# Swapping the queues of the two last stores, and loading the second weights in three pieces: a gated mix of a state-space scan and an MLP on one core

## The chip, the core and the metric

The kernel runs on one core of one Trainium2 chip. The metric is device microseconds of one execution. Executions of the same kernel in one comparison lie up to about 1.4 us apart (0.7%), and 2.3 us in one kernel of the experiments, so each comparison was run in rounds, with the kernel before and the new one in turn on the same chip. Ratios are the mean time of one kernel's fast runs over the mean of the other's in the same rounds, so they are not quite the ratio of the medians quoted beside them.

## The reference

`x` has 2048 rows of 640. Cut to what matters, with two parts and a gate per row:

```python
g = sigmoid((x * gate_w).sum(-1, keepdims=True))
a = ssm(x, Lambda, B, C, dt, Dskip)          # complex diagonal scan over 2048 rows, 640 states
b = gelu(x @ w1 + b1) @ w2 + b2              # 640 -> 1728 -> 640
out = g * a + (1 - g) * b                    # bfloat16, 2048 x 640
```

## The kernel before

The rows are worked in four chunks of 512. In each chunk TensorE makes the scan's inputs (`ssm`), the first MLP layer (`ff1`), the second MLP layer (`fin_b`) and the scan's output projection (`fin_a`). Loads are issued up front on the SP queue, in one long line; the load of the second weights `w2_sb` (the profile drops digits and calls it `w_sb`) is one instruction in that line:

```python
    nc.sync.dma_start_transpose(out=BT_re[:], in_=A_B_re[:, :])
    nc.sync.dma_start_transpose(out=BT_im[:], in_=A_B_im[:, :])
    nc.sync.dma_start_transpose(out=xT[1][:], in_=x2d[CH:2 * CH, :])
    nc.sync.dma_start_transpose(out=CT_re[:], in_=A_C_re[:, :])
    nc.sync.dma_start_transpose(out=CT_im[:], in_=A_C_im[:, :])
    nc.sync.dma_start(out=w2_sb[:, 0:KF - 1, :], in_=B_w2[0:(KF - 1) * P, :].rearrange("(kf p) d -> p kf d", p=P))
    # ... rest of w2 and b2, Dbc ...
    nc.sync.dma_start_transpose(out=xT[2][:], in_=x2d[2 * CH:3 * CH, :])
    nc.sync.dma_start_transpose(out=xT[3][:], in_=x2d[3 * CH:4 * CH, :])
    load_xn(0, H, TPC)
    load_xn(1)
```

The second layer reads it in 14 slices `kf`, one after the other (`fin_b`):

```python
            for d0, d1 in HALVES:
                p = bank()
                for kf in range(KF):
                    m = P if kf < KF - 1 else F_LAST + 1
                    nc.tensor.matmul(p[:, 0:d1 - d0], lhsT=gel[c][:m, kf, lo:lo + P], rhs=w2_sb[:m, kf, d0:d1],
                                     start=(kf == 0), stop=(kf == KF - 1))
```

The last output tile is cut into columns 0 to 320, 320 to 512 and 512 to 640, so that its end can leave early (`fin_a`). The first two cuts go out as one store of 128 KB, the last as one of 32 KB:

```python
                dve_now(ck.pe + 0.2, 0.45, f)          # f: the eviction, ot = bank * gate + gb
                if ti == NT - 1 and i > 0:
                    s0 = 0 if i == 1 else d0
                    q = nc.sync if i == 1 else nc.scalar
                    q.dma_start(out=out2d[ti * P:(ti + 1) * P, s0:d1], in_=ot[:, s0:d1])
```

Some terms first. An eviction is the instruction, of VectorE or ScalarE, that takes a finished result out of TensorE's bank; the last one of the kernel is VectorE's. A landing is the moment when the last increment of a DMA's completion semaphore is recorded. A drain is an instruction that reads and writes no tile; the closing part has some on every engine, and in the experiments empty ones are added to SP.

DMAs take their completion semaphore in turn from a small set, whichever queue they are on. After the program's last line there is a closing part that the framework adds: SP waits in a fixed order for the last DMA on each semaphore, and then all engines meet in two barriers.

## Time and profile before

| | before |
|---|---|
| device time, median of 3 runs | 217.63 us (217.43 to 217.79) |
| span in the profile | 216.2 us |
| TensorE busy | 211.9 us, 98% of the span |
| end of the last eviction to the end of the span | 2.66 us |

The stretches first. The columns are the stretch and its length, then the busy time of each engine with its number of instructions, the granted TensorE clock, the DMA engines' mean share, and GB/s:

```profile
core 0: us, PE busy (x) PEld busy (x) DVE busy (x) ACT busy (x) POOL busy (x), PEclk, DMA share, GB/s
22.50:213.20 190.70, 190.66 (x1228) 115.45 (x1228) 172.41 (x341) 76.37 (x130) 0.00 (x0) 1.00 0.24 59
```

TensorE is busy for 190.66 of these 190.70 us at full granted clock. Nothing that any other engine or a DMA does in this stretch can cost time unless it makes TensorE wait. The chain of work that ended last (start, length, what), shortened:

```profile
9.85 5.63 SPq L139
15.48 0.04 issue
15.52 6.92 DMA BT_im<-in_A_B_im_dram
22.45 0.05 issue
22.49 9.89 PE bank L478 x45
...
202.27 10.91 PE bank L544 x90
213.17 0.03 issue
213.20 0.35 DVE ot L549
```

Up to 22.45 us the chain is the SP queue's issues and the landing of BT_im; then it is TensorE to 213.17 us, and one eviction. The chain's list stops there, at 213.55 us; the span goes on to 216.21. That rest is the last store and the closing part.

The SP queue around the load of the second weights (L144):

```profile
30.03 0.58 SPq L144 DMA_DIRECT2D w_sb<-in_B_w_dram  x1
...
32.60 8.86 SPq L148 DMA_TRANSPOSE xT<-in_A_x_dram  x1
41.50 3.12 SPq L149 DMA_TRANSPOSE xT<-in_A_x_dram  x1
44.66 1.09 SPq L117 DMA_DIRECT2D xn<-in_A_x_dram  x2
45.88 1.20 SPq L299 DMA_TRANSPOSE gel<-gelN  x1
```

The load's semaphore is full at 39.3 us by the trace's landing records; its first reader runs at 57.65 us. The two last stores:

```profile
212.64 0.91 DVE L549 SCALAR_TENSOR_TENSOR ot<-bank,gcol,gb 128x192 bf16<-128x192 f32 x2 [0.27 <-PE bank L544]
212.72 0.44 PE L544 MATMUL bank<-CT_im,hs 128*128 128x128 bf16 x5
213.09 0.33 SPq L556 DMA_DIRECT2D out_dram<-ot  x1
213.58 0.38 ACTq L556 DMA_DIRECT2D out_dram<-ot  x1
```

The last instructions of SP, grouped by line (engine, operation and number; shortest, median and longest duration in ns; first and last start), and from the page the packets by which instructions are fetched:

```profile
L612 SPq EVENT_SEMAPHORE  x7: 17/28/28, 213.5 to 216.1; - x7
L612 SPq DRAIN  x3: 7/12/13, 215.3 to 216.0; - x3
```

```profile
q14 instruction: 5, 0.04, 0.1%
```

### The profile page before, as it was taken

How to read it: one execution, taken by the hardware profiler on the slowest of the kernel's cores; microseconds unless marked ns; L12 is line 12 of the kernel's file. 1: busy time of each engine (PE TensorE's matmuls, PEld its weight loads, DVE VectorE, ACT ScalarE, POOL GpSimd, SP SyncE). 2: the span in 40 equal slices, each digit the busy share in tenths (PEclk: the TensorE clock that was granted, in tenths of full speed). 3: DMA queues.
4: the chain of work that ended last, by engine and by line, in shares of the span. 5: the costliest groups of instructions: out<-in, count | busy, mean ns of one | idle time of the engine just before them, and what ended most of it. 6: DMA issues, size and time to landing. Idle time of an engine off the chain costs nothing.

```text
span 216.2 us, 3470 instructions
## 1 busy us (share of the span) xinstructions
PE 211.9 (98%) x1368; PEld 128.2 (59%) x1368; DVE 189.8 (88%) x393; ACT 91.7 (42%) x156; POOL 1.6 (1%) x12
## 2 busy tenths in 40 slices
PE   7999999999999999999999999999999999999994
PEld 3855444454577775444477777444457777777773
DVE  3889999999999899999999999999999999961152
ACT  3689456675696101556642200456662210022100
POOL 2000000000000000000000000000000000000000
PEclk9999999999999999999999999999999999999999
DMA  5999999995000042000010006100001000100011
GB/s 174 255 224 199 226 214 369 175 246 103 3 0 0 0 141 106 0 0 3 0 24 3 0 0 200 45 2 0 0 3 24 0 3 30 61 30 3 2 61 61
DMA packets 32339, 16.16 MB, mean 75 GB/s; under 512 B 25091, under 2 KB 32324, under 8 KB 32324
## 3 DMA queue, kind: packets, MB, share of 16 engines
q1 hardware_dynamic: 32114, 15.91, 30.2%
q8 instruction: 10, 0.16, 0.3%
q10 hardware_dynamic: 210, 0.04, 0.1%
q14 instruction: 5, 0.04, 0.1%
HBM read 7.24 MB, written 2.62 MB: 46 GB/s over the span
## 4 chain that ended last, share of the span: by engine, by line
PE 88%; SPq 5%; DMA 5%; issue 0%; DVE 0%
PE bank L525 28%; PE bank L544 20%; PE bank L478 20%; PE bank L267 19%; DMA BT_im<-in_A_B_im_dram 3%; SPq L139 3%; DMA xn<-in_A_x_dram 1%; SPq L127 1%; SPq L125 1%; PE bank L292 1%; SPq L124 0%; SPq L138 0%; DVE ot L549 0%
## 5 line engine op out<-in xcount | busy, mean ns | idle before, releaser
L525 PE MATMUL bank<-w_sb,gel 128*128 128x320 bf16 x448 | 61.6, 299 | 0.0
L525 PEld LDWEIGHTS <-gel 128*128 128x128 bf16 x448 | 43.6, 98 | 17.2
L481 ACT ACTIVATE bu<-bank 128x512 bf16<-128x512 f32 x40 | 23.9, 597 | 41.7 <-PE bank L478 41.7
L271 ACT ACTIVATE gel<-bank,colB 128x512 bf16<-128x512 f32 x52 | 34.6, 693 | 15.1 <-PE bank L267 14.8
L544 PEld LDWEIGHTS <-hs 128*128 128x128 bf16 x330 | 31.8, 98 | 11.9
L434 DVE TENSOR_TENSOR_SCAN g<-r_c,carry,v 128x512 bf16<-128x512 f32 x30 | 37.2, 1270 | 0.0
L528 ACT ACTIVATE gb<-bank,gcol 128x320 f32<-128x320 f32 x32 | 16.5, 527 | 48.2 <-PE bank L525 46.6
L267 PE MATMUL bank<-xT,w1b 128*128 128x512 bf16 x140 | 31.0, 379 | 0.0
L267 PE MATMUL bank<-xT,w1a 128*128 128x512 bf16 (+1 forms) x150 | 27.6, 344 | 0.0
L544 PE MATMUL bank<-CT_im,hs 128*128 128x320 bf16 (+2 forms) x165 | 27.1, 295 | 0.0
L544 PE MATMUL bank<-CT_re,hs 128*128 128x320 bf16 (+2 forms) x165 | 27.1, 295 | 0.0
L549 DVE SCALAR_TENSOR_TENSOR ot<-bank,gcol,gb 128x320 bf16<-128x320 f32 (+2 forms) x33 | 17.3, 533 | 9.5 <-PE bank L544 9.3
L478 PE MATMUL bank<-xT,BT_im 128*128 128x512 bf16 x100 | 24.9, 379 | 0.1
L478 PE MATMUL bank<-xT,BT_re 128*128 128x512 bf16 x100 | 24.8, 379 | 0.0
L267 PEld LDWEIGHTS <-w1b 128*128 128x128 bf16 x140 | 13.6, 98 | 16.3 <-DMA w1b<-in_B_w_dram 0.3
L267 PEld LDWEIGHTS <-w1a 128*128 128x128 bf16 x150 | 14.9, 100 | 11.7
L511 DVE TENSOR_TENSOR bank<-xn,Dbc 128x320 f32<-128x320 bf16 (+2 forms) x33 | 14.3, 483 | 5.8 <-ACT gb L528 5.8
L478 PEld LDWEIGHTS <-BT_im 128*128 128x128 bf16 x100 | 9.7, 98 | 12.2 <-DMA BT_im<-in_A_B_im_dram 0.6
L478 PEld LDWEIGHTS <-BT_re 128*128 128x128 bf16 x100 | 9.7, 98 | 11.0
L415 DVE TENSOR_TENSOR v<-wa,wb 128x512 bf16<-128x512 bf16 x40 | 15.2, 421 | 0.7
L415 DVE TENSOR_TENSOR wa<-TCOS,g 128x1024 bf16<-128x1024 bf16 x20 | 13.7, 686 | 0.1
L415 DVE TENSOR_TENSOR wb<-TSIN,g 128x1024 bf16<-128x1024 bf16 x20 | 13.7, 684 | 0.0
(98 smaller groups left out, 130.7 us busy)
## 6 DMA issues: line engine op xcount, KB each, us to landing
out_dram<-ot SPq DMA_DIRECT2D x15, 160.0 KB, 1.8
w_sb<-in_B_w_dram SPq DMA_DIRECT2D x1, 2080.0 KB
xn<-in_A_x_dram SPq DMA_DIRECT2D x3, 640.0 KB, 4.9
w1b<-in_B_w_dram SPq DMA_DIRECT2D x5, 240.0 KB, 4.2
w1a<-in_B_w_dram SPq DMA_DIRECT2D x5, 192.0 KB, 3.5
xn<-in_A_x_dram SPq DMA_DIRECT2D x2, 320.0 KB
Dbc<-in_A_Dskip_dram SPq DMA_DIRECT2D x1, 160.0 KB
out_dram<-ot SPq DMA_DIRECT2D x1, 128.0 KB
```

The lines of the kernel that those rows point to most:

```text
L139: nc.sync.dma_start_transpose(out=BT_re[:], in_=A_B_re[:, :])
L267: nc.tensor.matmul(p[:, t0:t1], lhsT=w, rhs=xT[c][:, kd, t0:t1], start=(kd == 0), stop=(kd == KD - 1))
L271: nc.scalar.activation(out=gel[c][:, kf, :], in_=p[:, :], func=ACT.Gelu_apprx_tanh, bias=b1_c[:, kf:kf + 1])
L415: nc.vector.tensor_tensor(out=o, in0=a, in1=b, op=op)
L434: nc.vector.tensor_tensor_scan(s["g"][:, ri, :], r_c[:, ks:ks + 1].to_broadcast([P, CH]), s["v"][:, ri, :], init, ALU.mult, ALU.add)
L478: nc.tensor.matmul(p[:], lhsT=BT[:, kd, ks * P:(ks + 1) * P], rhs=xT[c][:, kd, :], start=(kd == 0), stop=(kd == KD - 1))
L481: nc.scalar.activation(out=bu[:, ri, :], in_=p[:], func=ACT.Identity)
L511: dve_now(ck.pe, 0.45, lambda: nc.vector.tensor_tensor(out=p[:, 0:d1 - d0], in0=xn[c][:, a, d0:d1], in1=Dbc[:, d0:d1], op=ALU.mult))
L525: nc.tensor.matmul(p[:, 0:d1 - d0], lhsT=gel[c][:m, kf, lo:lo + P], rhs=w2_sb[:m, kf, d0:d1], start=(kf == 0), stop=(kf == KF - 1))
L528: nc.scalar.activation(out=gb[:, d0:d1], in_=p[:, 0:d1 - d0], func=ACT.Identity, scale=gcol[:, 1, ti:ti + 1])
L544: nc.tensor.matmul(p[:, 0:d1 - d0], lhsT=hs[c][:, j, lo:lo + P], rhs=CT[:, j % KS, d0:d1], start=False, stop=(j == 2 * KS - 1), skip_group ...
L549: nc.vector.scalar_tensor_tensor(out=ot[:, d0:d1], in0=p[:, 0:d1 - d0], scalar=gcol[:, 0, ti:ti + 1], in1=gbs[ti][:, d0:d1], op0=ALU.mult, ...
```

## The change

The intent: the last store, which ends the kernel, should leave from the queue with the cheaper issue; and the second weights should arrive piece by piece, so that a reader of the first slices need not wait for the last.

```diff
-    nc.sync.dma_start(out=w2_sb[:, 0:KF - 1, :], in_=B_w2[0:(KF - 1) * P, :].rearrange("(kf p) d -> p kf d", p=P))
+    for k0, k1 in ((0, 4), (4, 8), (8, KF - 1)):
+        nc.sync.dma_start(out=w2_sb[:, k0:k1, :], in_=B_w2[k0 * P:k1 * P, :].rearrange("(kf p) d -> p kf d", p=P))
...
-                    q = nc.sync if i == 1 else nc.scalar
+                    q = nc.scalar if i == 1 else nc.sync
```

## The prediction

> What bounds the kernel now. TensorE. The table of stretches gives it 190.66 us busy of the 190.70 us from 22.5 to 213.2 us, at a granted clock of 1.00; the chain of waits is TensorE alone from 22.49 to 213.17 us. Before that the chain is the first load and the SP queue's issues (L124 to L139) up to the landing of the transposed BT_im at 22.45 us. After it come a 0.35 us VectorE eviction, the last store and the closing handshake, to 216.2 us.
>
> Second weights. The one load (2080 KB) is issued at 30.03 us and takes 0.58 us of the SP queue. In the packet records its packets run from about 32 to 39 us and its semaphore is full at 39.4 us. The first matmul that reads it starts at 57.65 us: 18 us of slack, and the list of waits has no wait of TensorE for it. Three pieces move the same bytes in the same packets and add two issues; a plain load of 240 to 640 KB takes 0.37 to 0.55 us of the queue here, so my estimate is +0.6 us of SP issue time (0.5 to 1.0). Behind it stand the third and fourth xT (needed at 84 and 135 us), xn tiles, and the last gel tile of chunk 0, issued at 45.88, landed at about 50.2 and read at about 59.5 us: nine us of slack against 0.6. The third xT transpose holds the queue for 8.86 us because the second weights drain in front of it (the fourth took 3.12), so part of the added issue time disappears there. The chain up to 22.45 us is issued before this load and can't move. New TensorE waits for pieces two and three are for semaphores long full. Worth: 0.0 us.
>
> Swap of queues. Now the 128 KB piece goes out on SP at 213.09 us (issue 0.33 us; first packet after 0.83 us, last at 214.45), and the 32 KB piece on ACT at 213.58 us (issue 0.38 us; first packet after 0.89 us, last at 214.75; semaphore full at 215.09). The end follows that landing by 1.1 us. The Trainium skill ("DMA: Bandwidth & Descriptors", section "Issuing engines are not separate DMA queues") says that DMAs of both issuers run on the same 16 engines and that several issuers save only issue time; the trace agrees as far as both queues' packets follow without a gap (SP's last at 214.45, ACT's first at 214.48). So the swap moves only issue costs: the piece that ends the kernel gets the issue that is 0.05 us shorter, and starts about 0.06 us earlier; the large piece ends about 214.51, so the two now overlap by about 0.1 us on shared engines, which eats part of it. Worth: -0.05 to 0.0 us.
>
> Sum: 217.63 - 0.03 + 0.0 = 217.6 us. The three runs of before spread over 0.36 us, more than the effect. Range 217.1 to 218.2. Chances: faster by over 2% 0.01, within 2% 0.98, slower 0.01.
>
> What would show it right: TensorE gapless from 22.5 to 213.2 us; no wait on the second weights; the third xT's issue 0.5 to 1 us later but its landing within 1 us of before; the last store's issue on SP 0.33 us, landing near 215.05 us; span 216.1 to 216.3 us. Wrong: a TensorE wait at 57.6 or 59.5 us, or the 32 KB piece landing after 215.2 us.
>
> What would make it wrong: the two added loads shift which earlier DMA a later one shares its semaphore with, or the scheduler's order of loads and stores on SP, so that an issue waits near the end; or a large store issued from ACT starts much later than from SP.

## The result, and the profile after

| | before | after |
|---|---|---|
| device time, median of 4 runs each | 217.71 us | 217.95 us (217.77 to 218.27) |
| ratio, 95% interval | | 1.0012 (0.9994 to 1.0031) |
| span in the profile | 216.2 us | 216.5 us |
| end of the last eviction | 213.55 us | 213.62 us |
| from there to the last landing | 1.54 us | 1.49 us |
| from there to the end of the span | 2.66 us | 2.87 us |

The last two rows disagree: counted from the end of the last eviction, the last store landed 0.05 us earlier, and the kernel ended 0.21 us later.

The stretches after:

```profile
22.50:213.20 190.70, 190.16 (x1219) 115.45 (x1228) 172.38 (x340) 76.38 (x130) 0.00 (x0) 1.00 0.24 59
```

The 0.50 us of busy time that seem lost are nearly all not waits: 9 of the 1228 matmul records are missing from this trace (the weight loads, x1228 in both, are complete). In the chain each missing record leaves an "issue" piece of 0.05 us inside a run of TensorE work, as in the fourth to sixth line here; the rest is the later start:

```profile
15.54 6.99 DMA BT_im<-in_A_B_im_dram
22.52 0.05 issue
22.57 9.89 PE bank L479 x45
32.45 0.22 PE bank L268
32.67 0.05 issue
32.72 10.74 PE bank L268 x49
...
202.34 10.91 PE bank L545 x90
...
213.27 0.35 DVE ot L550
```

TensorE started its gapless stretch 0.08 us later (22.57 against 22.49, with the landing of BT_im, which is issued before anything that changed) and ended its last pieces 0.07 us later. In between nothing was lost. The SP queue around the load, now three instructions:

```profile
30.15 1.68 SPq L145 DMA_DIRECT2D w_sb<-in_B_w_dram  x3
...
33.76 7.63 SPq L149 DMA_TRANSPOSE xT<-in_A_x_dram  x1
41.44 3.20 SPq L150 DMA_TRANSPOSE xT<-in_A_x_dram  x1
44.69 1.09 SPq L117 DMA_DIRECT2D xn<-in_A_x_dram  x2
45.91 1.20 SPq L300 DMA_TRANSPOSE gel<-gelN  x1
```

The issues cost 1.10 us more (1.68 against 0.58). The third xT starts 1.16 us later and takes 1.23 us less, so that the fourth xT, at 41.44 us, is not late at all, and the gel tile behind it is 0.03 us late. The third xT itself lands at 44.17 us, before at 44.25. The two stores:

```profile
212.71 0.91 DVE L550 SCALAR_TENSOR_TENSOR ot<-bank,gcol,gb 128x192 bf16<-128x192 f32 x2 [0.28 <-PE bank L545]
212.79 0.44 PE L545 MATMUL bank<-CT_im,hs 128*128 128x128 bf16 x5
213.16 0.38 ACTq L557 DMA_DIRECT2D out_dram<-ot  x1
213.65 0.33 SPq L557 DMA_DIRECT2D out_dram<-ot  x1
```

The swap did what it should: 0.33 us of issue for the last piece instead of 0.38. And SP's closing instructions, with the instruction packets:

```profile
L613 SPq EVENT_SEMAPHORE  x7: 17/28/28, 214.0 to 216.4; - x7
L613 SPq DRAIN  x3: 7/7/120, 215.6 to 216.1; - x3
```

```profile
q14 instruction: 6, 0.05, 0.1%
```

One drain of SP now takes 120 ns where none took over 13, the first of them starts at 215.6 us instead of 215.3, and one more instruction packet falls within the span. The sign to go by is the late start. The long drain is not a sign of its own: in the runs below with added drains, the first of these takes 119 to 123 ns as well, right behind the issue of a load and without a gap before it. The single records of the two traces, in us from the end of the last eviction, worked out from their start times:

```
                                          before   after
SP's five waits for DMA semaphores, 1st    -0.09    0.42
                                    2nd     1.26    0.50
                                    3rd     1.55    0.57
                                    4th     1.62    1.33
                                    5th     1.71    1.51
the 32 KB store has landed                  1.54    1.49   (before: 3rd wait; after: 5th)
SP's drain after these waits                1.79    2.00
SP enters the first barrier                 1.85    2.18
VectorE leaves the first barrier            2.01    2.35
SP leaves the first barrier                 2.34    2.34
end of the span                             2.66    2.87
```

Three things differ. The landing is 0.05 us earlier. The landing is waited for fifth of five, so that nothing is left to wait for behind it; before it was third. And from SP's fifth wait to its entry into the barrier 0.68 us pass instead of 0.13. Before, a similar gap lies one step later, where SP leaves the barrier 0.33 us after VectorE does; there it costs less, because GpSimd is resetting semaphores at the same time (until 2.31 us after the eviction).

### The profile page after: what moved, and what is told of

Its sections match the earlier page's. It is cut to its first block, busy times and chain, and to the rows that moved or that the text cites. A ratio compares the mean times of both kernels' runs of the same rounds, so it can differ in the third digit from the quotient of the medians.

```text
span 216.5 us, 3461 instructions
## 1 busy us (share of the span) xinstructions
PE 211.3 (98%) x1357; PEld 128.2 (59%) x1368; DVE 189.3 (87%) x393; ACT 91.7 (42%) x156; POOL 1.6 (1%) x12
## 3 DMA queue, kind: packets, MB, share of 16 engines
HBM read 7.24 MB, written 2.62 MB: 46 GB/s over the span
## 4 chain that ended last, share of the span: by engine, by line
PE 88%; SPq 5%; DMA 5%; issue 0%; DVE 0%
PE bank L526 28%; PE bank L545 20%; PE bank L479 19%; PE bank L268 19%; DMA BT_im<-in_A_B_im_dram 3%; SPq L139 3%; DMA xn<-in_A_x_dram 1%; SPq L127 1%; SPq L125 1%; PE bank L293 1%; SPq L124 0%; SPq L138 0%; DVE ot L550 0%
## 5 line engine op out<-in xcount | busy, mean ns | idle before, releaser
L416 DVE TENSOR_TENSOR wb<-TSIN,bu 128x1024 bf16<-128x1024 bf16 x20 | 13.7, 685 | 0.0
```

What stands on the lines that cost most here:

```text
L416: nc.vector.tensor_tensor(out=o, in0=a, in1=b, op=op)
```

## The experiments

My first theory (A) was that a stall sits at a fixed place of SP's instruction stream, and that two more SP instructions push SP's closing drain behind it. The rivals were (B) that SP is slow to close because it has now issued the last store, and (C) that it is chance. Theory A was then set against a finer rival (A2): that not the place but the two added DMAs themselves, by number or by semaphore, cause it. A "late drain" is one of SP's closing drains that starts about 0.5 us after SP's last wait. Throughout, "end" is the time from the end of the last eviction to the end of the span. It is read from the traces and repeats to 0.02 us, while whole times scatter by 1 us.

### The two halves alone, and both kernels again

The swap alone:

```diff
-                    q = nc.sync if i == 1 else nc.scalar
+                    q = nc.scalar if i == 1 else nc.sync
```

> Only the queues of the two last pieces are swapped. In the profile of the changed kernel the last landing came 1.49 us after the end of the last eviction, 1.54 us in the kernel before, so the swap's own gain was 0.05 us; but the SP queue's closing drain started only 0.49 us after the wait for that landing, where it started 0.23 us after it before. Theory A (the late drain comes from the two added instructions on SP, which shift what follows them): here no late drain, ratio 0.999 to 1.000. Theory B (it comes from SP having issued the last store): late drain here too, span about 0.2 to 0.3 us longer, ratio 1.001. Theory C (chance of one profile): either, and not the same as in the changed kernel. All: TensorE as before from 22.5 to 213.2 us.

Measured: ratio 0.9996 (0.9977 to 1.0015). Last landing 1.48 us after the eviction, no late drain, end 2.61 us: 0.06 less than before. Theory B is out.

```profile
L612 SPq DRAIN  x3: 7/7/13, 215.5 to 216.1; - x3
```

The split alone:

```diff
-    nc.sync.dma_start(out=w2_sb[:, 0:KF - 1, :], ...)
+    for k0, k1 in ((0, 4), (4, 8), (8, KF - 1)):
+        nc.sync.dma_start(out=w2_sb[:, k0:k1, :], ...)
```

> Only the second weights in three pieces; stores as before. Theory A: the SP queue's closing drain is late (about 0.5 us after the last landing's wait) and the span 0.2 to 0.3 us longer, ratio 1.001. Theory B: no late drain, ratio 1.000, perhaps 0.1 us off the handshake because the last store's semaphore is now the last one SP waits for. All: three issues of together about 1.7 us instead of 0.58 on SP, third xT issue about 1.1 us later but landing within 1 us, no TensorE wait for the second weights.

Measured: ratio 1.0015 (0.9998 to 1.0032). Late drain, end 2.93 us: 0.27 more than before. The loss belongs to the split, at the far end of the kernel from where the split was made. No wait of TensorE for the second weights.

```profile
L613 SPq DRAIN  x3: 7/7/120, 215.8 to 216.2; - x3
```

The changed kernel and the kernel before, unedited:

> The changed kernel again, for a second profile of its end. Theories A and B: late drain again, ratio 1.001. Theory C: no late drain, span about 216.0 us, ratio 0.999 to 1.000.

> The kernel before against itself: the noise floor. Ratio 1.000 with an interval of about 0.002 either way; closing drain again about 0.23 us after the wait for the last landing under A and B, and under C sometimes later.

Measured: the changed kernel has ratio 1.0023 (1.0005 to 1.0041), the late drain and an end of 2.87 us again. The kernel before against itself has 1.0005 (0.9986 to 1.0024) and an end of 2.66 us again. Theory C is out. The whole time of the changed kernel is now clear of 1 by a little; its span in that profile is 0.9 us longer than that of the kernel before against itself, of which 0.21 is the end and the rest came before the last eviction, which ended at 213.81 and 213.08 us. That larger part is scatter of the start: in the latter profile no wait for BT_im stands in the chain at all.

### Two and eight empty instructions

Two empty drains on the SP queue, in the middle of the loads, in the kernel before:

```diff
+    for _ in range(2):
+        nc.sync.drain()
     nc.sync.dma_start_transpose(out=xT[2][:], in_=x2d[2 * CH:3 * CH, :])
```

> The kernel before with two empty drains added to the SP queue in the middle of the loads, and not one DMA more. So far the part of the span after the last eviction was 2.66 us before, 2.61 with the swap alone, 2.93 with the split alone, 2.87 with both. Theory A1 (the place of SP's closing instructions in its instruction stream decides: two more of any kind put a stall of about 0.4 us in front of its closing drain): drain about 0.5 us after SP's last wait instead of 0.075, end about 3.05 us after the last eviction (in this kernel the wait for the last landing is the third of five, so the drain starts later than in the split kernel), ratio 1.001 to 1.002. Theory A2 (the two added DMAs themselves, by their number or their semaphores): no stall, 2.66 us, ratio 1.000.

Measured: ratio 1.0027 (1.0012 to 1.0042), end 3.05 us. No DMA was added or moved; two empty instructions about 184 us before the end (33.2 us of 217.0) make the end 0.39 us longer. SP's closing drains:

```profile
L614 SPq DRAIN  x3: 7/7/106, 216.1 to 216.5; - x3
```

Theory A2 is out, and the place in the stream (A1) stands. The same with `range(8)`:

> The kernel before with eight empty drains on SP. Theory A1: the stall moves eight instructions forward in the stream, to before the last store, where SP waits for VectorE anyhow, so the closing part has none at all; in the kernel before it still lay between SP's closing drain and its last barrier wait (SP's barrier wait came 0.33 us after that of the other engines). End about 2.53 us after the last eviction, 0.13 us less than before, ratio 0.999 to 1.000. Theory A2: 2.66 us as before. If eight is worse than two (a stall that grows with the count), both fall.

Measured: ratio 0.9993 (0.9982 to 1.0005), end 2.51 us, 0.15 less than before. More instructions, shorter end: it is the place, not the count.

```profile
L614 SPq DRAIN  x3: 7/7/7, 216.0 to 216.3; - x3
```

The single records say the same. In the kernel before, the gap stands in front of SP's exit from the first barrier: 0.48 us after the end of the instruction before it. Two instructions earlier in SP's stream stands the first closing drain, and there all kernels with two more instructions have the gap, each time 0.47 us long. Eight earlier stands the last store on SP, which waits for VectorE anyhow; in the kernels with eight more no gap is left behind it.

The record of the instruction packet moves along. The last packet of 8192 bytes on queue 14 starts 2.97 us after the last eviction in the kernel before (after the span's end), 2.62 us in the changed kernel, 2.81 with two drains, and 0.96 us ahead of the end of the eviction with eight, where SP waits for VectorE anyhow. So the stall and this packet move together with the number of SP's instructions, which points to the fetching of SP's instructions but does not prove it. The Trainium skill ("Runtime: NRT & Kernel Launch", section "Instruction fetch mechanics") describes instruction memory refilled in 16 KiB blocks of 256 instructions and calls the crossing of a boundary "mostly hidden". Here the packets on this queue have 8192 bytes, and if the stall is such a crossing, it is hidden only where SP has something else to wait for. What happens inside the stall is not shown: the packet's record starts about 0.6 us after the late instruction (after the late barrier exit in the kernel before, after the late drain with two more instructions), so it is a companion of the stall and not proven to be what SP waited for.

### The changed kernel with six empty drains

The same edit with `range(6)` in the changed kernel brings it, too, to eight instructions more than before. It ran twice, the second time beside the changed kernel.

> The changed kernel with six empty drains on SP, so that it too stands eight instructions further than before. Theory A1: the stall leaves the closing part; the gain of the swap (0.05 us) and of the semaphore order (the last landing is awaited fifth of five, not third, about 0.15 us) come out: end about 2.33 us after the last eviction, against 2.87 in the changed kernel and 2.66 before; ratio to before 0.998 to 0.9995. Theory A2: 2.87 us and ratio 1.001 to 1.002 as in the changed kernel.

> The changed kernel a third time, beside its padded version. Stall in front of SP's closing drain, end 2.87 us after the last eviction, ratio to before 1.001 to 1.002.

> The changed kernel with six empty drains on SP again, as the best version so far. End 2.32 us after the last eviction, 0.34 us less than before and 0.55 less than the changed kernel; ratio to before 0.9985 (0.997 to 1.0), to the changed kernel of the same rounds about 0.9975.

Measured: padded, ratio to before 0.9987 (0.9968 to 1.0007) and 0.9996 (0.9981 to 1.0011), end 2.32 us in both profiles. The changed kernel beside it: 1.0010 (0.9995 to 1.0026), end 2.86 us. So the end is 0.34 us shorter than before and 0.54 us shorter than unpadded. The whole times are in line with that but don't resolve it: the expected ratio of 0.9975 between the two came out as 0.9996 / 1.0010 = 0.9986. It is the version with the shortest end, and by the whole time no proven winner.

### What the split is worth when the load is late

The prediction called the load's slack 18 us. To test that, and to see what a split can do, the load was moved from the SP queue to ACT, behind the evictions of the second chunk's second state block:

```diff
-    nc.sync.dma_start(out=w2_sb[:, 0:KF - 1, :], ...)
...
+            if c == 1 and ks == 1:
+                for k0, k1 in ((0, KF - 1),):      # or the three pieces
+                    nc.scalar.dma_start(out=w2_sb[:, k0:k1, :], in_=B_w2[k0 * P:k1 * P, :].rearrange("(kf p) d -> p kf d", p=P))
             scan_ops(c, ks, bu, ck.act)
```

In one piece:

> The load of the second weights, in one piece, is taken off the SP queue and issued by ACT in the second chunk's state-space stage, at about 52 us instead of 30 us (a test of what its slack is worth, not a proposal). If the 18 us of slack are real, an issue 22 us later must run out of them: estimate from the packet rate before (about 290 packets of 1280 bytes per us, 1664 packets, first packet 0.9 us after the issue): landing near 59 us, a TensorE wait of about 1.3 us (0.7 to 2.0) at 57.7 us, carried to the end, since TensorE is gapless from there on: ratio about 1.006. If TensorE had other slack later, less.

Measured: issued at 51.02 us, landed at 59.26 us, 19.9 us later than before, and TensorE waits 1.9 us:

```profile
PE bank L527 <- DMA w_sb<-in_B_w_dram: 1.9, 1, 1.9
```

A landing 19.9 us later for a wait of 1.9 us makes the slack about 18 us, as read. The ratio, 1.0154 (1.0119 to 1.0189), is larger than expected. The six runs fall in two groups: three with spans of 217.9 to 218.5 us and mean granted clocks of 0.998 to 1.0, and three with 219.8 to 220.2 us and 0.992. A clock lower by 0.8% over 218 us makes 1.7 us, about the distance of the groups. The first group alone is about 2.4 us above the kernel before, of which the profile shows 1.9 us as the wait; the other half microsecond stays open. I ran it once more to catch a profile of the second group:

> The one-piece late load once more, for a profile. Its six runs fell in two groups: three with a mean granted clock of 0.998 to 1.0 and spans of 217.9 to 218.5 us, three with 0.992 and spans of 219.8 to 220.2 us; the profile was of the first group. If the second group is a fall of the granted clock after the wait for the second weights, a profile of it shows the granted clock below 1 in the stretch just after about 59 us and 1.0 elsewhere, 1.7 us longer in all. By chance (about one half) this profile is of the first group again, and then the question stays open.

Measured: 220.39 us in a single run (the kernel before 217.64), span 218.6 us, clock 1.000, wait 2.2 us. By its clock it is of the first group, so where in those three runs the clock fell stays open.

In three pieces:

> The same late issue from ACT, but in the three pieces of the change. If the pieces land one after the other, the first (512 packets) lands near 55 us, before its first matmul, the third near 59 us and is first read about 1.1 us after 57.7: TensorE waits 0 to 0.4 us, ratio 1.000 to 1.002: the split then pays for what it is meant for. If the pieces are served side by side and all land near 59 us: as with one piece, ratio about 1.006.

Measured: ratio 1.0047 (1.0031 to 1.0064). The pieces land at 55.70, 57.51 and 59.69 us, one after the other. TensorE starts on time, does the eight slices of the first two pieces, and waits for the third:

```profile
57.61 1.25 PE L527 MATMUL bank<-w_sb,gel 128*128 128x320 bf16 x8
59.73 10.51 PE L527 MATMUL bank<-w_sb,gel 128*128 128x320 bf16 x76 [0.87 <-DMA w_sb<-in_B_w_dram]
```

The wait is 0.87 us, not the 0 to 0.4 expected: the last piece landed 0.4 us later than the one load did, with three issues on ACT of together 1.51 us instead of 0.40. So the split works as intended, halving the wait, where there is a wait. The Trainium skill ("Perfetto Trace Analysis", section "DMA Optimizations") says that splitting a DMA may let some of it start sooner; in this pair no transfer started sooner (the first piece was issued at 51.34 us, the one load at 51.02), but the first reader did, at 57.61 us instead of 59.30. The changed kernel adds that it is worth nothing where the reader comes 18 us after the landing.

Both kernels have as many SP instructions as the kernel before, and this separates the third effect. With one piece the last landing is awaited third and the end is 2.67 us; with three pieces the semaphores have rotated by two, it is awaited fifth, and the end is 2.50 us. The order of SP's waits is worth 0.17 us here.

## Why the prediction was right or wrong

The ends of the kernels, with the three terms:

| kernel | SP instructions against before | last landing awaited | last store on | end, us |
|---|---|---|---|---|
| before (twice) | 0 | third | ACT | 2.66 |
| swap alone | 0 | third | SP | 2.61 |
| late, three pieces | 0 | fifth | ACT | 2.50 |
| two drains | +2 | third | ACT | 3.05 |
| split alone | +2 | fifth | ACT | 2.93 |
| changed (three times) | +2 | fifth | SP | 2.86 to 2.87 |
| eight drains | +8 | third | ACT | 2.51 |
| changed, six drains (twice) | +8 | fifth | SP | 2.32 |

Two instructions more cost 0.39 us (3.05 - 2.66), the order of the waits gives back 0.12 us (2.93 - 3.05), and the swap 0.06 us: 2.66 + 0.39 - 0.12 - 0.06 = 2.87 us, as measured.

- **The bound, right.** TensorE stayed gapless from about 22.5 to 213.2 us.
- **"Worth: 0.0 us" of the second weights, right for the load, wrong for the kernel.** There was no wait at 57.6 or 59.5 us, and the slack was confirmed at about 18 us. The step that failed is the silent one in the sum, "+ 0.0": I counted the added SP issues only for what stands behind them in the line of loads. They also move every later SP instruction along its stream, and this cost 0.39 us at the other end, less 0.12 from the rotation of the semaphores. I had named a shift in the sharing of semaphores as a danger, in that an issue might wait near the end. No issue did; the shift changed the order of SP's closing waits, and that helped.
- **The added issue time, mis-sized.** "+0.6 us (0.5 to 1.0)" measured 1.10 us: each of the two added issues took 0.51 us and a gap of 0.04 us. The prediction's own 0.37 to 0.55 us per load, taken twice, would have given 0.7 to 1.1. That it would disappear in the third xT was right: nothing behind it was issued more than 0.03 us late. (The gel tile behind it landed at 51.2 us in the kernel before, not at 50.2 as the prediction has it; that is another load's landing. Its slack was 8 us and not 9, and nothing hung on it.) With the load gone from the line, in the late one-piece kernel, the same transpose took 4.10 us instead of 8.86, as the reason given asked for.
- **The swap, right.** "-0.05 to 0.0 us" was 0.06 us by the end and 0.05 to 0.06 us by the landing. The trace agrees with what the Trainium skill's section named there says of issue time: the first packets follow the end of the issue by 0.50 to 0.52 us on either queue in these two profiles, and only the issue time differs.
- **"The end follows that landing by 1.1 us", the term that was mis-sized.** I took the closing part for a constant. It is 1.12 us before and 1.38 us after (2.87 - 1.49), and 0.83 us in the padded kernel. In the profiled run this and the start, 0.07 us later, put the span at 216.5 us, where "216.1 to 216.3" was predicted; the other three runs had 216.0 to 216.2.
- **The total, right.** 217.95 us against 217.6 (217.1 to 218.2). There is luck in this: the range is 1.1 us wide, several times all that the change did, and two terms that it did not have, +0.39 and -0.12 us, partly cancelled. That the direction was missed doesn't show in a single comparison with this scatter; it took the traces and the two-drain run to see it.

## What to carry to other kernels

Before splitting a load, look up when it lands and when it is first read: with 18 us between, a split can only add, and with a wait it helped by half. When a change looks neutral and the traces agree everywhere but in the last 3 us, compare the closing part instruction by instruction: the number of instructions on an issuing queue and the order in which it waits for its DMAs together moved this kernel's end by 0.7 us between the worst and the best version. Such a gain is fragile, since the next edit of that queue moves it again, so it is the last thing to tune and never the verdict on a change.

## What the Trainium skill lacked or had wrong

- "Runtime: NRT & Kernel Launch", section "Instruction fetch mechanics": it gives 16 KiB blocks of 256 instructions and calls the boundary mostly hidden. Here queue 14 fetched 8192 bytes at a time (queue 8 fetched 16384). A stall that moves with such a packet, and may be that boundary, cost SP about 0.55 us between its last wait and the barrier (0.68 us against 0.13 us), 0.39 us of the whole end.
- No page says that the number of instructions on an issuing queue can move a stall into or out of the closing part. Two empty instructions made the end 0.39 us longer, eight made it 0.15 us shorter.
- No page says that the order of the closing waits for DMA semaphores counts. The last landing awaited fifth instead of third was worth 0.12 to 0.17 us.
- "Perfetto Trace Analysis", section "DMA Optimizations": its advice on splitting names idle DMA engines as the condition, but not that a reader must be waiting. With 18 us of slack the split was worth nothing, and with a wait of 1.9 us it left 0.9 us.
- "DMA: Bandwidth & Descriptors", section "Latency and other measured facts": about 0.6 us to the first byte for these queues, without saying from where it counts. In the kernel before, the first packet's record came 0.83 us (SP) and 0.89 us (ACT) after the start of the issue, 0.50 and 0.51 us after its end.
